# Low halves of split operands and the gate's products moved from GpSimd to VectorE in an attention, mixing and feed-forward kernel

## The chip, the cores and the metric

The kernel runs on one core of one Trainium2 chip. The metric is device time in microseconds from launch to end; three runs of the kernel before took 486.18, 487.32 and 492.7 us, median 487.32 us. The engines are called by their short names: PE (TensorE matmul), PEld (its weight load), DVE (VectorE), ACT (ScalarE), POOL (GpSimd) and SP (the queue that issues all DMAs here).

## The reference

Three stages on 2 batches of 768 tokens, 8 heads of 64, model width 512, all in float32:

```python
# attention: local window of 96 keys plus the first 8 keys, linear distance bias
scores = q @ k^T / 8 - slope[h] * dist
a = softmax(where(is_global | is_local, scores, -1e9));  x = a @ v
# mixing
theta = x @ w_theta;  zr, zi = x * cos(theta), x * sin(theta)
u = x + w_tok_r @ zr + w_tok_i @ zi          # over tokens
x2 = u + max(u @ w_ch, 0)
# feed forward
h = max(x2 @ w_in, 0)                        # width 1024
gate = 1 / (1 + exp(-conv3(h)))              # depthwise over tokens, 3 taps
out = (h * gate) @ w_out
```

## The kernel before

**Numbers.** PE multiplies in a shortened float32 format. So an operand that needs full precision is split: its *high half* is the value copied into that format (`Net.hi`, line 79 on ACT, 81 on POOL, 83 on DVE), its *low half* is the value minus the high half (`Net.lo`, line 87, on POOL or DVE). A product of two split operands is three matmuls: high by high, low by high, high by low. A low half can only be computed once its high half is written. Line 87 is one helper for all of them, so in the profile the tile names tell which split it is.

**Weights** come as float64 and are turned into float32 on the chip, block by block, by a queue of small steps (`Net.weight`, lines 110 to 136): *load* (SP, into one of two buffers `wst`), *a* (ACT, line 95), *b* (DVE, lines 100 and 101), *c* (DVE, lines 107 and 108; afterwards the load buffer is free), *d* (high half, ACT) and *e* (low half, POOL). `advance` (lines 138 to 148) puts the steps of three neighbouring blocks into one queue, and `run(k)` takes k of them out between other work. There are 48 blocks: 4 of `w_theta`, 24 of `w_tok` (384 columns each), 4 of `w_ch`, 8 of `w_in`, 8 of `w_out` (512 columns each).

**The order of the work** is written out by hand: a manual schedule, every engine runs its instructions in the order in which the program emits them and waits at each for what it needs.

- *Attention* (`run_fast`, line 811 on): 48 steps, three per (batch, head), each two tiles of 128 queries. A step emits scores (PE), the biased scores and their row minimum (DVE, line 297), the exponential (ACT), transposes and products with v (PE), each some steps behind the other. Once per head the next head's keys and queries are split (lines 839 and 840): for keys the high half on ACT and the low half on POOL, for queries the high half on DVE and the low half on POOL. Weight steps of `w_theta` and of eight `w_tok` blocks run in between.
- *Mixing* (`Mix.tail`, line 596 on): the angles (`reduce_theta`, lines 456 and 457 on DVE), then for each token tile sine and cosine (ACT), their products with x (DVE, line 470), high halves (DVE) and low halves (POOL) of these: this is `trig`. Then token mixing `tok` in four parts (batch 0 and 1 by first and second half of the outputs, 144 matmuls of 384 columns each), with the rest of the `w_tok` blocks prepared meanwhile; its end adds x (DVE, line 517). Then u is split (`u_split`), and `ch` does the channel mixing in 16 tiles, each with a maximum and sum (DVE, line 542), a high half (ACT) and a low half (POOL).
- *Feed forward*: `ff_in` does 24 matmuls for each of 16 (batch, block of 128 channels). Behind it runs `gate` in stages that a `Pipe` moves by one each time: maximum with 0 into one of three buffers `h` (ACT, line 566); three convolution taps (DVE, lines 568 to 570); sigmoid (ACT, line 572) and its product with h (line 574, POOL for even blocks, DVE for odd ones); high half (ACT) and low half (POOL). A buffer `h` is free again once its product has read it. Last, `ff_out` does 12 tiles of 24 matmuls of 512 columns, batch 0 first, copies them out of PSUM and stores them.

Of the kernel before, what the change touches and what calls it, by code (L numbers as in the profile page):

```python
# [21 lines left out]
P = 128  # L22
# [15 lines left out]
TURN = 6.283185  # the float32 next below 2 pi: half a turn stays inside Sin's range  # L38
# [8 lines left out]
F64_LOW = f32_of_bits(0x38000000)  # high word of the float64 2^-127, read as float32  # L47
F64_HIGH = f32_of_bits(0x47EFFFFF)  # high word of float32's largest value


class Net:
# [41 lines left out]
    def f64_a(self, w, t):  # L93
        """w [P, 2n] int32: pairs of words of float64; t = the high words' magnitudes."""
        self.nc.scalar.activation(t.bitcast(F32), w[:, 1 : w.shape[1] : 2].bitcast(F32), AF.Abs)  # L95

    def f64_b(self, w, t):
        """Into float32's range, and the exponent's and fraction's bits to their places."""
# [4 lines left out]
    def f64_c(self, w, t):  # L103
        """The low word's top bits, the sign and the exponent's top bit."""
# [5 lines left out]
    def weight(self, src, width, hi, lo, eh="A", el="P"):  # L110
        """Queue the load of a block of weights, its conversion and its split. The queue's
        steps are ordered so that a step's inputs come from steps well before it."""
# [25 lines left out]
    def advance(self, n):  # L138
        j = self.jobs

        def put(i, *steps):
            if 0 <= i < len(j):
                self.bg.extend(j[i][x] for x in steps)

        put(n - 1, 1)
        put(n - 2, 2, 3)
        put(n, 0)
        put(n - 2, 4, 5)

    def drain(self):  # L150
        """No more weights soon: queue what the last ones still lack."""
        n = len(self.jobs)
        self.advance(n)
        self.advance(n + 1)
        self.jobs = []
# [11 lines left out]
class Pipe:  # L167
    """Chains of dependent operations, one stage a step, so that no engine waits for
    what another was only just given."""
# [10 lines left out]
    def add(self, *new):  # L180
        """The first stages at once."""
# [14 lines left out]
class Attention:  # L196
    """Attention of one (batch, head) at a time, its inputs split ahead of use."""
# [57 lines left out]
class FastAttention(Attention):  # L255
    """1 <= n_local <= 121 and n_global <= 8: each tile of 128 queries meets the
    120 keys before it, the first 8 keys and its own 128 keys."""
# [6 lines left out]
    def table(self, i):  # L264
        """The head's biases; tile 0's window has its own."""
# [73 lines left out]
class GeneralAttention(Attention):  # L339
    """Any n_global and n_local: every query tile meets all keys."""  # L340
# [44 lines left out]
class Mix:  # L385
    """What follows the attention."""
# [20 lines left out]
    def transpose_x(self, b, c, e="A"):  # L407
        """x^T of a pair of heads, in stages."""
# [9 lines left out]
    def split_xT(self, b, c, el="P"):  # L418
# [6 lines left out]
    def theta(self, t, tag, bufs):  # L425
        """The products of one token tile, one at a time."""
# [11 lines left out]
    def theta1_open(self, t):  # L438
        """Theta of batch 1's token tile t as far as the first three pairs of heads go."""
# [10 lines left out]
    def reduce_theta(self, th, out):  # L450
        """theta in turns, less the nearest whole number of them; in stages."""
# [7 lines left out]
    def trig(self, b, t, r, z, em, eh, el):  # L459
        """z = x cos, x sin of one token tile, split; z: [cos, sin] of [P, hi/lo, DM]; in stages."""  # L460
# [17 lines left out]
    def trig0(self):  # L478
        """x cos and x sin of batch 0, in stages."""
# [3 lines left out]
        for k in range(NT + 2):  # L483
# [4 lines left out]
            if k < NT:  # L488
                tr.append(self.trig(0, k, self.r[:, k], z[k], "VV", "VV", "PP"))
# [5 lines left out]
    def load_tok(self, hf, part, eh="A", el="P"):  # L495
        """Queue the weights of token tiles 2 part, 2 part + 1 (r, i each) for one half of the outputs."""
# [6 lines left out]
    def tok(self, b, hf, m, s, bank):  # L503
        """Add token tile s's part of y^T, rows m."""
# [511 lines left out]
```

## Time and profile before

| What | Value |
|---|---|
| runs (median) | 486.18, 487.32, 492.7 us (487.32) |
| span of the profiled execution, first to last instruction | 484.6 us |
| busy: PE, PEld, DVE, ACT, POOL | 420.3, 388.4, 418.1, 217.2, 251.7 us |
| mean granted TensorE clock | 0.952 of full |

The profile lists one execution by its span alone; its own device time is not among the numbers given, so the span is what its rows are laid against. The span begins with the first instruction and ends with the last, and the median of the runs is 2.7 us above it. "Busy" is the time in which an engine had an instruction under way; a wait inside an instruction (for a port, for instance) counts as busy, a wait for a semaphore before it does not. Times of matmuls overlap, so a row of many is read by its sum and not by one of them.

### The profile page before, as it was taken

Reading aid. Unit: us, or ns where it says so; the run is one execution under the profiler, and the core shown is the slowest. Engines: PE = TensorE matmul, PEld = TensorE weight load, DVE = VectorE, ACT = ScalarE, POOL = GpSimd, SP = SyncE. Lnnn points to the kernel's source line nnn. Section 1 sums busy time; section 2 is a strip of 40 time slices with the busy share of each in tenths; the row PEclk is TensorE's granted clock in tenths of the full one; section 3 lists DMA queues with packets and bytes.
Section 4 is the critical chain, followed back from the end, with each engine's and each line's share of the span. In section 5 each row is a group of like instructions: output and inputs, shape, how many; then the busy total and the mean of one; then the engine's idle time right before and its main releaser. Section 6 shows DMA issues by size and latency. Waiting matters only on the chain.

```text
span 484.6 us, 6636 instructions
## 1 busy us (share of the span) xinstructions
PE 420.3 (87%) x2376; PEld 388.4 (80%) x2376; DVE 418.1 (86%) x700; ACT 217.2 (45%) x420; POOL 251.7 (52%) x164
## 2 busy tenths in 40 slices
PE   3888797889899897799668999679999688999995
PEld 2778797778797797799557999479999688788885
DVE  5989999999998997998788999999999999994000
ACT  3867767556678303902323222544634433443000
POOL 2756666654544742674233285577556675575000
PEclk9979979798999998999998999979999898999999
DMA  6865545534320003102444423312311000003111
GB/s 216 297 219 190 177 158 193 161 133 164 93 67 1 0 1 98 32 1 76 120 131 131 130 88 122 94 45 87 105 38 34 0 1 0 1 0 123 52 43 50
DMA packets 14297, 44.53 MB, mean 92 GB/s; under 512 B 1840, under 2 KB 2352, under 8 KB 14256
## 3 DMA queue, kind: packets, MB, share of 16 engines
q1 hardware_dynamic: 14256, 44.03, 28.1%
q8 instruction: 20, 0.33, 0.3%
q14 instruction: 21, 0.17, 0.1%
HBM read 40.88 MB, written 3.15 MB: 91 GB/s over the span
## 4 chain that ended last, share of the span: by engine, by line
DVE 39%; PE 17%; DMA 6%; issue 4%; ACT 1%; SPq 0%; ACTq 0%; DVEq 0%
PE O L90 6%; DVE wbit L107 5%; DMA wst<-w_tok 4%; DVE wbit L101 4%; PE PT L90 4%; PE S L90 4%; DVE wbit L108 4%; DVE c L569 4%; DVE wbit L100 3%; DVE c L570 3%; DVE r L470 3%; PE X L90 3%; DVE scratch L470 3%; DVE c L568 2%; PE TH L90 2%
## 5 line engine op out<-in xcount | busy, mean ns | idle before, releaser
L87 POOL TENSOR_TENSOR qk<-a,qk 128x768 fp32r<-128x768 f32 (+1 forms) x29 | 58.5, 2017 | 40.7 <-ACT qk L79 27.2
L90 PE MATMUL S<-qk 128*128 128x256 f32 (+1 forms) x192 | 39.5, 332 | 26.3 <-DVE nm L297 10.5
L95 ACT ACTIVATE wbit<-wst 128x512 f32<-128x512 f32 (+1 forms) x48 | 29.4, 616 | 73.0 <-DMA wst<-w_tok 25.5
L90 PEld LDWEIGHTS S<-qk 128*128 128x128 f32 x192 | 31.1, 220 | 31.4 <-issue 13.6
L87 POOL TENSOR_TENSOR wt<-wbit,wt 128x384 fp32r<-128x384 f32 x24 | 27.6, 1150 | 54.2 <-ACT wt L79 54.2
L306 ACT ACTIVATE a<-a,nm 128x256 f32<-128x256 f32 (+1 forms) x96 | 42.0, 484 | 23.9 <-DVE nm L297 23.8
L100 DVE TENSOR_SCALAR wbit<-wbit 128x512 f32<-128x512 f32 (+1 forms) x48 | 40.7, 848 | 7.4 <-ACT wbit L95 7.3
L107 DVE SCALAR_TENSOR_TENSOR wbit<-wst,wbit 128x512 int32<-128x512 int32 (+1 forms) x48 | 45.5, 949 | 1.2
L101 DVE TENSOR_SCALAR wbit<-wbit 128x512 int32<-128x512 int32 (+1 forms) x48 | 44.3, 923 | 1.7
L90 PE MATMUL O<-wt,z 128*128 128x384 f32 x144 | 33.0, 362 | 13.5 <-ACT wt L79 9.0
L90 PEld LDWEIGHTS O<-wt,z 128*128 128x128 f32 x144 | 25.8, 197 | 18.6 <-ACT wt L79 11.5
L87 POOL TENSOR_TENSOR g<-c,g 128x768 fp32r<-128x768 f32 x16 | 34.3, 2148 | 9.9 <-ACT g L79 8.0
L108 DVE SCALAR_TENSOR_TENSOR wbit<-wst,wbit 128x512 int32<-128x512 int32 (+1 forms) x48 | 36.1, 753 | 1.7
L297 DVE CUSTOM_DVE_ANT_0 a<-S,a 128x256 f32<-128x256 f32 (+1 forms) x96 | 34.1, 394 | 1.2 <-PE PT L315 0.8
L79 ACT ACTIVATE wt<-wbit 128x384 fp32r<-128x384 f32 x24 | 12.5, 520 | 44.4 <-DVE wbit L108 44.0
L90 PE MATMUL O<-a,a 128*128 128x65 f32 x236 | 31.9, 280 | 0.0
L574 POOL TENSOR_TENSOR c<-c,scratch 128x768 f32<-128x768 f32 x8 | 18.9, 2364 | 23.4 <-ACT c L572 23.4
L90 PEld LDWEIGHTS O<-a,a 128*128 128x128 f32 x236 | 31.0, 204 | 0.0
L315 PE MATMUL PT<-ident,a 128*128 128x128 f32 x176 | 30.0, 294 | 0.0
L570 DVE SCALAR_TENSOR_TENSOR c<-scratch,cwt,c 128x767 f32<-128x767 f32 x16 | 28.0, 1750 | 0.6
L90 PE MATMUL TH<-wth,xTs 128*128 128x512 f32 x96 | 28.3, 436 | 0.2
L79 ACT ACTIVATE a<-PT 128x512 f32<-128x512 f32 (+1 forms) x48 | 26.2, 546 | 2.8 <-PE PT L315 2.8
(193 smaller groups left out, 1077.2 us busy)
## 6 DMA issues: line engine op xcount, KB each, us to landing
a<-qk SPq DMA_DIRECT2D x14, 792.0 KB, 4.8
wst<-w_tok SPq DMA_DIRECT2D x24, 384.0 KB, 3.1
a<-v SPq DMA_DIRECT2D x16, 357.5 KB, 2.9
wst<-w_in SPq DMA_DIRECT2D x8, 512.0 KB, 3.4
wst<-w_out SPq DMA_DIRECT2D x8, 512.0 KB, 3.5
out<-scratch SPq DMA_DIRECT2D x11, 256.0 KB, 2.6
wst<-w_theta SPq DMA_DIRECT2D x4, 512.0 KB, 5.5
wst<-w_ch SPq DMA_DIRECT2D x4, 512.0 KB, 3.5
```

The source lines that it names most:

```text
L79: self.nc.scalar.activation(out, in_, AF.Copy)
L87: e.tensor_tensor(out, in_, hi.bitcast(F32), op=ALU.subtract)
L90: self.nc.tensor.matmul(out, l, r, start=start, stop=stop)
L95: self.nc.scalar.activation(t.bitcast(F32), w[:, 1 : w.shape[1] : 2].bitcast(F32), AF.Abs)
L100: nc.vector.tensor_scalar(t.bitcast(F32), t.bitcast(F32), F64_LOW, F64_HIGH, op0=ALU.max, op1=ALU.min)
L101: nc.vector.tensor_scalar(t, t, 3, 0x3FFFFFFF, op0=ALU.logical_shift_left, op1=ALU.bitwise_and)
L107: nc.vector.scalar_tensor_tensor(t, lo, 29, t, op0=ALU.logical_shift_right, op1=ALU.bitwise_or)
L108: nc.vector.scalar_tensor_tensor(t, hi, -(1 << 30), t, op0=ALU.bitwise_and, op1=ALU.bitwise_or)
L297: nc.vector.tensor_tensor_reduce(sS[:, c], s["sp"][:, c], self.T[1 if t0 else 0], scale=-0.125, scalar=3.0e38, op0=ALU.add, op1=ALU.min, a ...
L306: self.nc.scalar.activation(sS[:, rng[u]], sS[:, rng[u]], AF.Exp, bias=nm[:, u : u + 1], scale=-1.0)
L315: self.nc.tensor.transpose(pt[:, c], sS[:, c], net.head["ident"])
L570: nc.vector.scalar_tensor_tensor(c[:, 0 : S - 1], h[:, 1:S], cw[:, f, 2:3], c[:, 0 : S - 1], op0=ALU.mult, op1=ALU.add)
```

## The change

Every low half that POOL computed is computed by DVE: the defaults and arguments `"P"` become `"V"`. So are the gate's products of even blocks. POOL keeps what it does once at the start (index patterns, constants). For three kinds of work the low half is also emitted later than before: in the weight queue, step *e* of a block is put at the head of the next `advance` (so `drain` advances once more); in `ch` and in `gate` a `yield` stands between high and low half, which puts the low half one `Pipe` step later. No shape, buffer, tile, DMA or matmul changes. The diff also takes out comments, which moves line numbers by 2 to 4 (the convolution taps are lines 571 to 573 there, the product 577).

```diff
-    def weight(self, src, width, hi, lo, eh="A", el="P"):
+    def weight(self, src, width, hi, lo, eh="A", el="V"):
...
+        put(n - 3, 5)
         put(n - 1, 1)
         put(n - 2, 2, 3)
         put(n, 0)
-        put(n - 2, 4, 5)
+        put(n - 2, 4)
...
         self.advance(n)
         self.advance(n + 1)
+        self.advance(n + 2)
...
-    def split_xT(self, b, c, el="P"):
+    def split_xT(self, b, c, el="V"):
...
-                tr.append(self.trig(0, k, self.r[:, k], z[k], "VV", "VV", "PP"))
+                tr.append(self.trig(0, k, self.r[:, k], z[k], "VV", "VV", "VV"))
...
-    def load_tok(self, hf, part, eh="A", el="P"):
+    def load_tok(self, hf, part, eh="A", el="V"):
...
             n.hi(eh, self.x2[b][0][:, m, c], x2)
+            yield
             n.lo(el, self.x2[b][1][:, m, c], x2, self.x2[b][0][:, m, c])
...
         n.hi(eh, g[:, 0], c)
+        yield
         n.lo(el, g[:, 1], c, g[:, 0])
...
-        tr = [self.trig(1, s, r[s], self.z[1][s], "VV", "VV", "PP") for s in range(NT)]
+        tr = [self.trig(1, s, r[s], self.z[1][s], "VV", "VV", "VV") for s in range(NT)]
...
-        pipe.step(*(self.u_split(0, x, 0, "V", "P") for x in range(KC)))
+        pipe.step(*(self.u_split(0, x, 0, "V", "V") for x in range(KC)))
...
-                    new = [self.ch(b, hf, m, bank(), "A", "P")]
+                    new = [self.ch(b, hf, m, bank(), "A", "V")]
...
-            pipe.step(self.gate(b, f, hs[k % 3], cs[:, k % 4], banks, "PV"[f % 2], "A", "P"))
+            pipe.step(self.gate(b, f, hs[k % 3], cs[:, k % 4], banks, "V", "A", "V"))
...
-                split_q(net, st, qk, "A", "P")
+                split_q(net, st, qk, "A", "V")
             if i > 0 and tp == 0:
-                split_k(net, st, qk, "A", "P")
-                split_q(net, st, qk, "V", "P")
+                split_k(net, st, qk, "A", "V")
+                split_q(net, st, qk, "V", "V")
...
-            last.add(mix.split_xT(b, c, "P" if b else "V"))
+            last.add(mix.split_xT(b, c, "V"))
...
-        net.lo("P", qk0[:, S : 2 * S][:, qc[x]], q[:, qc[x]], qk0[:, qc[x]])
+        net.lo("V", qk0[:, S : 2 * S][:, qc[x]], q[:, qc[x]], qk0[:, qc[x]])
```

Three places show how the change moves instructions. First DVE in `trig` of batch 1 (`r` and `scratch` hold sine and cosine, `z` the split products; `xs` is x), before:

```order
L470 TENSOR_TENSOR r_147<-r_147,xs_134 128x512
L470 TENSOR_TENSOR scratch<-scratch,xs_134 128x512
L83 CAST z_1842<-r_147 128x512
L83 CAST z_1842<-scratch 128x512
L470 TENSOR_TENSOR r_147<-r_147,xs_134 128x512
```

and with the change:

```order
L472 TENSOR_TENSOR r_147<-r_147,xs_134 128x512
L472 TENSOR_TENSOR scratch<-scratch,xs_134 128x512
L83 CAST z_1842<-r_147 128x512
L83 CAST z_1842<-scratch 128x512
L87 TENSOR_TENSOR z_1842<-r_147,z_1842 128x512
L87 TENSOR_TENSOR z_1842<-scratch,z_1842 128x512
L472 TENSOR_TENSOR r_147<-r_147,xs_134 128x512
```

The two low halves now stand between one token tile's high halves and the next tile's products. Second DVE while the `w_tok` blocks of the second output half are prepared (`wbit` is a block under conversion, `wst` its load buffer, `wt` the split weights), before:

```order
L107 SCALAR_TENSOR_TENSOR wbit_2077<-wst_2075,wbit_2077 128x384
L108 SCALAR_TENSOR_TENSOR wbit_2077<-wst_2075,wbit_2077 128x384
L100 TENSOR_SCALAR wbit_2081<-wbit_2081 128x384
L101 TENSOR_SCALAR wbit_2081<-wbit_2081 128x384
L107 SCALAR_TENSOR_TENSOR wbit_2081<-wst_2079,wbit_2081 128x384
```

and with the change:

```order
L107 SCALAR_TENSOR_TENSOR wbit_2077<-wst_2075,wbit_2077 128x384
L108 SCALAR_TENSOR_TENSOR wbit_2077<-wst_2075,wbit_2077 128x384
L87 TENSOR_TENSOR wt_2073<-wbit_2077,wt_2073 128x384
L100 TENSOR_SCALAR wbit_2081<-wbit_2081 128x384
L101 TENSOR_SCALAR wbit_2081<-wbit_2081 128x384
L107 SCALAR_TENSOR_TENSOR wbit_2081<-wst_2079,wbit_2081 128x384
```

The low half of a block stands right behind its last conversion step on DVE, although ACT's copy into the high half lies between the two, and ahead of the next block's conversion. Third DVE in the feed-forward stage once the weights are done (`c` is the convolution, its buffer numbers left equal; `scratch` holds h, `g` the split gate), before:

```order
L568 TENSOR_SCALAR c_3037<-scratch,cwt 128x768
L569 SCALAR_TENSOR_TENSOR c_3037<-scratch,cwt,c_3037 128x767
L570 SCALAR_TENSOR_TENSOR c_3037<-scratch,cwt,c_3037 128x767
L574 TENSOR_TENSOR c_3037<-c_3037,scratch 128x768
L568 TENSOR_SCALAR c_3037<-scratch,cwt 128x768
```

and with the change:

```order
L571 TENSOR_SCALAR c_3035<-scratch,cwt 128x768
L572 SCALAR_TENSOR_TENSOR c_3035<-scratch,cwt,c_3035 128x767
L573 SCALAR_TENSOR_TENSOR c_3035<-scratch,cwt,c_3035 128x767
L577 TENSOR_TENSOR c_3035<-c_3035,scratch 128x768
L87 TENSOR_TENSOR g_3376<-c_3035,g_3376 128x768
L571 TENSOR_SCALAR c_3035<-scratch,cwt 128x768
```

Before, the product stands on DVE behind every second block's taps only; now it stands behind every block's, and behind it the low half of the block two further back.

## Rows read from the trace of the kernel before

**Rows 1.** Page, part 1: busy us, share of the span, instructions.
```profile
PE 420.3 (87%) x2376; PEld 388.4 (80%) x2376; DVE 418.1 (86%) x700; ACT 217.2 (45%) x420; POOL 251.7 (52%) x164
```
**Rows 2.** Page, part 4: the chain that ended last, shares by engine.
```profile
DVE 39%; PE 17%; DMA 6%; issue 4%; ACT 1%; SPq 0%; ACTq 0%; DVEq 0%
```
**Rows 3.** Busy time by stretch: us, PE, PEld, DVE, ACT, POOL, clock, DMA.
```profile
10.00:142.60 132.60, 113.35 (x788) 106.17 (x789) 127.84 (x352) 91.33 (x197) 76.24 (x42) 0.91 0.53 175
...
153.00:218.00 65.00, 58.48 (x301) 54.09 (x301) 61.58 (x80) 23.54 (x42) 37.39 (x27) 0.97 0.08 25
218.00:258.00 40.00, 31.58 (x167) 28.06 (x165) 33.15 (x51) 10.64 (x21) 14.46 (x13) 1.00 0.39 112
258.00:318.00 60.00, 50.47 (x271) 48.31 (x271) 56.94 (x79) 20.38 (x37) 32.28 (x25) 0.95 0.34 105
...
343.50:412.90 69.40, 62.25 (x335) 60.80 (x333) 68.21 (x57) 29.80 (x52) 40.16 (x19) 0.95 0.07 23
```
**Rows 4.** Timeline, gate stage: start us, duration us, engine, line, operation.
```profile
419.18 2.14 POOL L87 TENSOR_TENSOR g<-c,g 128x768 fp32r<-128x768 f32 x1 [0.38 <-ACT g L79]
419.66 2.48 DVE L570 SCALAR_TENSOR_TENSOR c<-scratch,cwt,c 128x767 f32<-128x767 f32 x1
422.07 0.94 DVE L574 TENSOR_TENSOR c<-c,scratch 128x768 f32<-128x768 f32 x1
422.94 0.60 DVE L568 TENSOR_SCALAR c<-scratch,cwt 128x768 f32<-128x768 f32 x1
...
424.63 1.02 DVE L570 SCALAR_TENSOR_TENSOR c<-scratch,cwt,c 128x767 f32<-128x767 f32 x1
```
**Rows 5.** Groups on DVE, attention (10 to 142.6 us): count, busy us, mean ns, idle.
```profile
L267 DVE TENSOR_SCALAR a<-Dt 128x256 f32<-128x256 f32 x16 | 11.4, 710 | 1.0 <-issue 0.5
L100 DVE TENSOR_SCALAR wbit<-wbit 128x384 f32<-128x384 f32 x8 | 9.7, 1211 | 0.0
...
L101 DVE TENSOR_SCALAR wbit<-wbit 128x384 int32<-128x384 int32 x8 | 8.1, 1009 | 0.3
...
L100 DVE TENSOR_SCALAR wbit<-wbit 128x512 f32<-128x512 f32 x4 | 6.8, 1690 | 0.0
```
**Rows 6.** Groups on POOL, the same stretch.
```profile
L87 POOL TENSOR_TENSOR qk<-a,qk 64x816 fp32r<-64x816 f32 x14 | 29.4, 2098 | 30.4 <-ACT qk L79 23.4 <-issue 3.1 <-PE PT L315 2.1
L87 POOL TENSOR_TENSOR qk<-a,qk 128x768 fp32r<-128x768 f32 x15 | 29.1, 1941 | 10.3 <-DVE qk L83 6.0 <-ACT qk L79 3.8
```
**Rows 7.** Timeline, DVE in `trig` of batch 1.
```profile
195.57 0.68 DVE L470 TENSOR_TENSOR r<-r,xs 128x512 f32<-128x512 f32 x1
...
196.78 0.42 DVE L83 CAST z<-r 128x512 fp32r<-128x512 f32 x1
...
197.45 1.78 DVE L470 TENSOR_TENSOR r<-r,xs 128x512 f32<-128x512 f32 x1
...
201.50 1.78 DVE L470 TENSOR_TENSOR r<-r,xs 128x512 f32<-128x512 f32 x1
```
**Rows 8.** Timeline, one `w_tok` block after another, second output half.
```profile
238.18 0.54 ACT L95 ACTIVATE wbit<-wst 128x384 f32<-128x384 f32 x1 [2.64 <-DMA wst<-w_tok]
...
239.15 0.36 DVE L101 TENSOR_SCALAR wbit<-wbit 128x384 int32<-128x384 int32 x1
...
240.81 0.56 DVE L108 SCALAR_TENSOR_TENSOR wbit<-wst,wbit 128x384 int32<-128x384 int32 x1
...
241.40 0.53 ACT L79 ACTIVATE wt<-wbit 128x384 fp32r<-128x384 f32 x1
...
242.01 1.02 POOL L87 TENSOR_TENSOR wt<-wbit,wt 128x384 fp32r<-128x384 f32 x1 [1.65 <-ACT wt L79]
242.19 1.26 DVE L107 SCALAR_TENSOR_TENSOR wbit<-wst,wbit 128x384 int32<-128x384 int32 x1
```
**Rows 9.** Chain of waits, in order of time: end of `ch`, start of `ff_out`.
```profile
332.85 2.09 PE PT L90 x12
...
412.96 11.27 PE O L90 x48
```

More of the change, by code (lines that the diff above doesn't have):

```diff
@@ L724, in tail @@
                 self.tok(1, 1, m, s, pb)
-            pipe.step(*(self.u_split(0, x, 1, "V", "P") for x in range(KC) if m == 0))
+            pipe.step(*(self.u_split(0, x, 1, "V", "V") for x in range(KC) if m == 0))
             n.run(12)
@@ L878, in run_general @@
         split_k(net, st, qk, "V", "P")
-        split_q(net, st, qk, "V", "P")
+        split_q(net, st, qk, "V", "V")
         o = net.bank("O", 2)
```

## The prediction

> **What bounds the kernel now.** I start with the busy times [rows 1]. DVE has something under way in 86% of the span and PE in 87%, but PE's matmuls overlap, and a wait inside one counts as busy, so its share says less. The chain of waits puts 39% on DVE and 17% on PE [rows 2]; the reader is to see that DVE leads and that POOL, busy for 251.7 us, is not on it at all. The table by stretch then says where: DVE is busy 127.8 of 132.6 us in the attention, 61.6 of 65.0 in the stretch with `trig`, 56.9 of 60.0 before and in the channel mixing, 68.2 of 69.4 in the gate stage [rows 3]. Only from 218 to 258 us is nobody full: there the `w_tok` blocks come one after another and the queue of load, ACT and DVE sets the pace. After 412.96 us PE does `ff_out` without a gap [rows 9]; nothing of the change shortens that.
>
> The next question is what DVE's busy time is made of. In the gate stage the timeline shows the same convolution tap taking 2.48 us at 419.66, while a low half runs on POOL from 419.18 for 2.14 us, and 1.02 us at 424.63, with POOL idle [rows 4]. The tap does not run slower beside POOL: its 2.48 are nearly the 1.66 us that POOL still had to go and then its own 1.02. So DVE and POOL take turns whenever both read SBUF this way, and the wait is booked as DVE busy. The same two values appear for the products in `trig` (0.68 and 1.78 us [rows 7]) and for the conversion steps (0.36 alone, means of 1.0 to 1.7 in the attention [rows 8, 5]). That is the whole case for the change: DVE already pays for POOL's work, at POOL's price of about 2.1 us for 768 columns, where DVE itself does a two-input operation of that size in 0.94 us [rows 4, 6].
>
> A rule speaks against it. The Trainium skill (Perfetto Trace Analysis, "Optimizing Scalar/DVE Operations") says that when DVE is saturated, work may be moved off it, even to GpSimd, and adds that the two share a read port, so that it might not help. By its first half the attention alone, where DVE has no room [rows 3], would grow by the 36.2 us of added work that is counted below, and the kernel would take 523 us; the turn-taking in the timeline [rows 4] sides with its second half.
>
> **Part by part.** Durations come from one profiled execution of 484.6 us span; the median of the runs, 487.3, is 2.7 above it. The terms are differences, so I carry them over to the median.
>
> *Attention, 10 to 142.6 us.* POOL's 14 key and 15 query low halves [rows 6] come to DVE: 14 x 1.0 (0.94 scaled to 816 columns) and 15 x 0.94 = 28.1. Eight `w_tok` and four `w_theta` low halves add 8 x 0.56 and 4 x 0.68 (two-input operations of 384 and 512 columns [rows 8, 7]) = 7.2, and one low half of x^T 0.9: 36.2. What goes is the holding [rows 5]: line 267, 11.4 less 16 x 0.36 = 5.6 (0.36 is what 384 columns take alone [rows 8], so a bound for its 256); lines 100 and 101 at 384 columns, 17.8 less 16 x 0.36 = 12.0; line 100 at 512 columns, 6.8 less 4 x 0.48 (0.36 scaled) = 4.9. That is 22.5 in four rows; line 101 at 512 columns, the casts and the low halves of x^T already on DVE are held too and not in it. Independent DVE operations also start before the last one ends: two products take 1.21 us from start to start and 1.36 by duration [rows 7], which takes about 0.07 off each of 43 added ones, 3.0 in all. So the stretch changes by at most 36.2 - 22.5 - 3.0 = +10.7 and by less than nothing if the unlisted forms are held like the listed ones (then they give more than 10.7). I take **0**, nearer to the second end because every held form in the rows loses most of its time, and keep -6 and +10.7.
>
> *`trig` and the blocks around it, 153 to 218 us.* A held token tile takes 4.05 us on DVE (197.45 to 201.50). With the change it is two products in 1.21, two casts in 0.67 (196.78 to 197.45), two low halves like the products, 1.21: 3.09 [rows 7]. That is 0.96 less. Twelve tiles pass here; some, like the one at 195.57, are not held now and gain nothing on DVE, but the held first tile of batch 1 also lets PE start earlier. I count seven: **-6.7**, with ends of -3 (few held) and -9.
>
> *`w_tok` blocks of the second half, 218 to 258 us.* Here the change adds a wait. On DVE the low half stands directly behind line 108, and it needs ACT's copy: 108 ends at 241.37, the copy ends at 241.93, POOL starts at 242.01, so 0.64 us pass in which DVE stands still, and behind it stands the next block's conversion, and behind that the next load, which needs the buffer. Then the low half itself, 0.56. Now DVE goes ahead at once and is held instead for 1.26 - 0.56 = 0.70 [rows 8]. So a turn costs 1.20 in place of 0.70, 0.5 more; two blocks are under way, so twelve blocks are six turns, and the first has its loads early: 5 x 0.5 = 2.5, less two holds of 0.70 that the first pair loses. **+1.1**, ends -1 and +5. Nothing on SP moves past anything: the queue of steps keeps its order, the low half only changes its place from the end of one `advance` to the head of the next.
>
> *258 to 318 us.* DVE would do twelve 512-column blocks at 2 x 0.48 and 3 x 0.68 (3.0 each, 36.0), nine sums of `tok` at 0.56 (5.0), eight casts at 0.3 (a 512-column one follows the next by 0.33 [rows 7]; 2.4), fourteen low halves of u and x2 at 0.56 (7.8), five of line 542 (2.8) and small ones (1.3): 55.3, less 0.07 x 85 = 6.0 for overlap. Six handovers of 0.64, where the low half stands directly behind 108, give +3.8, and its idle 3.1 [rows 3] stays: 56.2 against 60. The loads can set the pace instead (ACT waits 2.64 for one [rows 8]), so I take less than the 3.8: **-1.5**, ends -5 and +4.
>
> *318 to 343.5 us.* Low halves of x2 and `w_out` come in, holds go out: 0.
>
> *Gate stage.* Now DVE goes from its first tap at 343.5, where I cut the stretch, to the product of block 9 at its end; then ACT can fill that block's h again, its PSUM bank comes free and `ff_out` starts at 412.96. With the change a block's taps take 1.69 from the first's start to the third's (422.94 to 424.63) and 1.02, so 2.71; the product 0.87 (422.07 to 422.94), a low half of the same size the same [rows 4]. Up to that product stand 11 blocks' taps, 10 products, 8 low halves, four `w_out` blocks of 3.0 and the low half of a fifth: 29.8 + 8.7 + 7.0 + 12.7 = 58.2, so it is done at 401.7, and ACT's 0.5 or so later `ff_out` can start. PE says about the same: `ff_in` starts at 334.94 and needs 16 x 24 matmuls at 2.09 per 12, 66.9 us, so until 401.8 [rows 9]. Against 412.96 that is **-10.6**, ends -5 (if handovers to ACT stall the gate) and -11.1 (PE's floor). The extra stage of the pipe costs nothing: batch 1's last low half is needed only when six tiles of `ff_out`, 33 us at 11.27 for two [rows 9], are done.
>
> Sum: 0 - 6.7 + 1.1 - 1.5 - 10.6 = -17.7, so **469.6 us** (span near 467).
>
> **The rivals.**
> (a) *The attention pays.* The listed holds are most of what there is, and the key low half waits for ACT's copy of the keys once per head. Then the attention costs +8, the `w_tok` blocks +5 in place of +1.1: 481. For it: the listed rows cover 22.5 of 36.2 only. Against: every DVE form that I looked at and that reads SBUF shows two values. Within 2%; chance 0.14.
> (b) *The attention gains too.* If all forms are held like those in rows 5 and overlap is full, its -6 and two more in 258 to 318 make 462. Chance 0.14.
> (c) *Slower: DVE inherits POOL's waits.* ACT takes the next block's line 95 before it copies the last block, and line 95 waits for a load (2.64 us [rows 8]). Where DVE has other work ready at that moment, in the 24 blocks of 512 columns after the attention, the low half holds all of it up for 2.64 in place of 0.64: 24 x 2.0 = 48, so 517 or 518. Nine such blocks use up the gain; at 14, 28 us, it is slower by 2%. For it: in-order DVE and POOL's long waits for ACT [rows 6]. Against: loads start when DVE frees a buffer, two steps ahead, and the blocks stand further apart where other work is emitted between. Chance 0.07.
> (d) *No relief: the long durations are not POOL's doing*, so that added work adds up: 523 from the attention alone. It is where the rule's first half would lead. Against it rows 4. Chance 0.03.
>
> **How the numbers follow.** My forecast has 0.62. Within 2% means 477.6 to 497.1, about what a measurement of this kernel can tell from no change. The forecast's own ends leave 0.02 of it above 477.6; so faster 0.60 + 0.14 = 0.74; within 2% 0.02 + 0.14 + 0.01 (a weak (c)) = 0.17; slower 0.06 + 0.03 = 0.09. The range goes from 457 (b with its ends) to 481 (the middle of a): it leaves out (c), (d), half of (a) and the end of (b), 0.2.
>
> **What would show it.** Right: POOL has nothing after its first microseconds; line 100, 101 and the taps show one value each (0.36 to 0.48, 1.02); DVE's busy time falls to about 400 although it has some 150 more instructions; `ff_in` runs without a gap and `ff_out` starts near 395; a token tile of `trig` takes 3.1 us. Wrong: taps over 1.1 us without POOL; DVE idle behind ACT's copies for more than 20 us in sum; an attention that ends later than 150 us; a gap on PE before `ch` of batch 1 that grows by more than what was won before it.

## The result, and the profile after

The changed kernel takes 467.17 us (median of four runs, 465.49 to 469.67), the kernel before beside it 486.75: a ratio of 0.9588 (95% interval 0.9522 to 0.9653), 20 us less. The profiled execution has a span of 463.6 us in place of 484.6. A second profiled execution of the changed kernel (e5) has 462.9 us at a mean granted clock of 0.961 (0.981 in the first, 0.952 before), so the gain does not hang on the clock's mean. Executions of one kernel differ by up to some 1.5%, in e9 with the clock that they were granted (452.1 to 453.5 us at 0.981 to 0.984, 458.8 to 459.2 at 0.966 to 0.973), and all ratios, and the times given for e7 and e9, leave out those more than 1.5% above the kernel's fastest.

Parts 1 and 4 of the page after, to lay beside [rows 1, 2]:

```profile
PE 411.5 (89%) x2376; PEld 380.5 (82%) x2376; DVE 383.3 (83%) x854; ACT 217.6 (47%) x420; POOL 1.4 (0%) x10
...
DVE 46%; PE 37%; DMA 7%; ACT 4%; issue 3%; SPq 0%; ACTq 0%; DVEq 0%
```

DVE executes 154 instructions more and is busy 34.8 us less. The shares of the chain must not be laid side by side: before, it could be followed back only to 153.9 us (its shares add up to 67%), after to 8.9. From the second tile of `trig` on, which both cover, DVE has 187 us of the chain before and 101 after, PE 83 and 154; behind the gate's first tap DVE has 65 us before and 0.4 after. DVE no longer leads everywhere.

Where the 21.0 us of the span come from, by landmark instructions (us; the end of the last row minimum and of the last conversion step, the start of the last product of `trig` and of the first matmul of `ff_in` and `ff_out`):

| Stretch | before | after | difference |
|---|---|---|---|
| start to the last row minimum of the attention | 142.64 | 144.89 | +2.3 |
| to the start of the last product of `trig` | 72.9 | 64.9 | -8.0 |
| to the last conversion step of `w_tok` | 42.3 | 41.4 | -0.9 |
| to the start of `ff_in` | 77.0 | 74.0 | -2.9 |
| `ff_in`, to the start of `ff_out` | 78.2 | 67.2 | -11.0 |
| to the end | 71.6 | 71.2 | -0.4 |

The last product of `trig` was itself held before (1.77 us) and is not after (0.69). To its end, `trig` gains 9.1 us and the `w_tok` blocks lose 0.2.

The groups on DVE in the attention, for [rows 5] and the added low halves:

```profile
L87 DVE TENSOR_TENSOR qk<-a,qk 64x816 fp32r<-64x816 f32 x15 | 15.1, 1005 | 0.7 <-ACT qk L79 0.3
L87 DVE TENSOR_TENSOR qk<-a,qk 128x768 fp32r<-128x768 f32 x15 | 14.4, 959 | 0.5
...
L269 DVE TENSOR_SCALAR a<-Dt 128x256 f32<-128x256 f32 x15 | 4.4, 294 | 0.5
...
L101 DVE TENSOR_SCALAR wbit<-wbit 128x384 int32<-128x384 int32 x8 | 2.9, 360 | 0.3
L100 DVE TENSOR_SCALAR wbit<-wbit 128x384 f32<-128x384 f32 x8 | 2.8, 353 | 0.0
...
L100 DVE TENSOR_SCALAR wbit<-wbit 128x512 f32<-128x512 f32 x4 | 1.7, 423 | 0.0
```

The held forms fell to what they take alone (1211 to 353 ns, 1690 to 423). That pays for the 29.5 us of key and query low halves: the four rows of [rows 5] give back about 24 us, and forms that they leave out some more (line 101 at 512 columns 7.7 to 1.7 us, the low halves of x^T 8.2 to 3.8).

The gate stage's timeline on DVE, for [rows 4], and the chain of waits there, for [rows 9]:

```profile
363.28 0.61 DVE L571 TENSOR_SCALAR c<-scratch,cwt 128x768 f32<-128x768 f32 x1
363.93 1.02 DVE L572 SCALAR_TENSOR_TENSOR c<-scratch,cwt,c 128x767 f32<-128x767 f32 x1
364.98 1.02 DVE L573 SCALAR_TENSOR_TENSOR c<-scratch,cwt,c 128x767 f32<-128x767 f32 x1
365.91 0.95 DVE L577 TENSOR_TENSOR c<-c,scratch 128x768 f32<-128x768 f32 x1
366.78 0.95 DVE L87 TENSOR_TENSOR g<-c,g 128x768 fp32r<-128x768 f32 x1
```

```profile
390.42 2.12 PE PT L90 x12
392.54 11.02 PE O L90 x48
```

A block's five operations take 4.4 us with both taps at 1.02, and PE goes from `ff_in` to `ff_out` without a gap. The table by stretch (columns as in [rows 3]) shows the same, and where somebody is still not full:

```profile
10.00:142.60 132.60, 110.96 (x779) 101.86 (x780) 125.26 (x381) 90.66 (x194) 0.00 (x0) 0.96 0.52 174
153.00:212.40 59.40, 58.05 (x310) 54.25 (x310) 55.30 (x110) 25.74 (x46) 0.00 (x0) 1.00 0.09 28
212.40:252.00 39.60, 31.27 (x169) 28.50 (x167) 28.45 (x62) 11.20 (x23) 0.00 (x0) 1.00 0.40 113
...
335.50:392.50 57.00, 57.00 (x327) 57.00 (x326) 55.64 (x73) 30.52 (x51) 0.00 (x0) 1.00 0.07 22
```

In the `w_tok` blocks DVE is busy 28.5 of 39.6 us. The timeline there shows the wait that the change added, for [rows 8] (in brackets the idle time before, and who ended it):

```profile
217.43 0.55 ACT L95 ACTIVATE wbit<-wst 128x384 f32<-128x384 f32 x1 [2.69 <-DMA wst<-w_tok]
217.88 0.51 ACT L79 ACTIVATE wt<-wbit 128x384 fp32r<-128x384 f32 x1
218.42 0.56 DVE L87 TENSOR_TENSOR wt<-wbit,wt 128x384 fp32r<-128x384 f32 x1 [1.24 <-ACT wt L79]
```

ACT takes the next block's line 95 first, which waits for its load; the copy of the finished block stands behind it, and DVE behind that. The wait is not 1.24 us each time: over the whole kernel DVE waits 12.7 us in 16 waits for ACT's copies of `w_tok`, 18.5 us with those of other weights and of the keys and queries.

### The profile page after: what moved, and what is told of

The parts are those of the page before. It is cut to its first block, busy times and chain, and to the rows that moved or that the text cites. A ratio compares the mean times of both kernels' runs of the same rounds, so it can differ in the third digit from the quotient of the medians.

```text
span 463.6 us, 6488 instructions
## 1 busy us (share of the span) xinstructions
PE 411.5 (89%) x2376; PEld 380.5 (82%) x2376; DVE 383.3 (83%) x854; ACT 217.6 (47%) x420; POOL 1.4 (0%) x10
## 4 chain that ended last, share of the span: by engine, by line
DVE 46%; PE 37%; DMA 7%; ACT 4%; issue 3%; SPq 0%; ACTq 0%; DVEq 0%
PE O L90 11%; PE S L90 8%; PE PT L90 8%; DVE qk L87 6%; DVE a L299 6%; PE X L90 5%; DVE wbit L107 4%; PE TH L90 4%; DMA wst<-w_tok 3%; DVE wbit L108 3%; DVE z L87 3%; DMA wst<-w_in 3%; DVE wbit L101 2%; DVE wbit L100 2%; DVE qk L83 2%
## 5 line engine op out<-in xcount | busy, mean ns | idle before, releaser
L90 PE MATMUL O<-wt,z 128*128 128x384 f32 x144 | 30.1, 345 | 9.5 <-ACT wt L79 9.5
L108 DVE SCALAR_TENSOR_TENSOR wbit<-wst,wbit 128x512 int32<-128x512 int32 (+1 forms) x48 | 30.0, 625 | 1.7
L107 DVE SCALAR_TENSOR_TENSOR wbit<-wst,wbit 128x512 int32<-128x512 int32 (+1 forms) x48 | 30.0, 624 | 1.5
L87 DVE TENSOR_TENSOR qk<-a,qk 64x816 fp32r<-64x816 f32 (+1 forms) x30 | 29.5, 982 | 1.2 <-ACT qk L79 0.3
L90 PE MATMUL TH<-wth,xTs 128*128 128x512 f32 x96 | 26.0, 408 | 0.5 <-ACT r L456 0.2
L90 PE MATMUL PT<-wt,z 128*128 128x384 f32 x132 | 25.8, 335 | 0.0
L87 DVE TENSOR_TENSOR wt<-wbit,wt 128x384 fp32r<-128x384 f32 x24 | 13.3, 556 | 12.7 <-ACT wt L79 12.7
L90 PEld LDWEIGHTS PT<-wt,z 128*128 128x128 f32 x132 | 23.2, 188 | 0.0
L317 PEld LDWEIGHTS PT<-ident,a 128*128 128x128 f32 x176 | 22.4, 151 | 0.7 <-ACT a L79 0.7
L90 PE MATMUL S<-wt,z 128*128 128x384 f32 x120 | 22.3, 337 | 0.5 <-DVE z L87 0.5
L90 PEld LDWEIGHTS S<-wt,z 128*128 128x128 f32 x120 | 20.9, 188 | 0.8 <-DVE z L87 0.8
```

Source lines behind the costliest of these rows:

```text
L87: e.tensor_tensor(out, in_, hi.bitcast(F32), op=ALU.subtract)
L90: self.nc.tensor.matmul(out, l, r, start=start, stop=stop)
L107: nc.vector.scalar_tensor_tensor(t, lo, 29, t, op0=ALU.logical_shift_right, op1=ALU.bitwise_or)
L108: nc.vector.scalar_tensor_tensor(t, hi, -(1 << 30), t, op0=ALU.bitwise_and, op1=ALU.bitwise_or)
L317: self.nc.tensor.transpose(pt[:, c], sS[:, c], net.head["ident"])
```

## The experiments

The theory: while a two-input operation ran on POOL, DVE was *held* (its instruction was under way but waited), and the gain is the holding that goes, mostly in `trig` and the gate. The rivals: the later emission is the gain; or it comes from the gate alone; or the long durations on DVE were not POOL's. The stages of every profiled execution, by the landmarks of the table above (one execution each, us):

| Kernel | row minimum | `trig` | `w_tok` | to `ff_in` | `ff_in` | ratio to before (95%) |
|---|---|---|---|---|---|---|
| before | 142.6 | 72.9 | 42.3 | 77.0 | 78.2 | 1 |
| after, again (e5) | 144.6 | 65.7 | 41.2 | 72.9 | 67.2 | 0.9568 (0.9496 to 0.9640) |
| e1, gate only | 142.5 | 72.9 | 42.8 | 76.3 | 67.9 | 0.9793 (0.9753 to 0.9833) |
| e2, delay only | 143.0 | 73.0 | 42.2 | 76.9 | 79.0 | 1.0024 (0.9993 to 1.0055) |
| e3, no delay | 145.7 | 64.9 | 41.4 | 80.3 | 68.4 | 0.9734 (0.9703 to 0.9766) |
| e4, POOL load | 144.8 | 65.7 | 41.4 | 73.0 | 78.2 | one run, 476.39 us |
| e6, attention on POOL | 146.1 | 64.9 | 41.1 | 73.0 | 67.2 | 0.9485 (0.9445 to 0.9524) |
| e7, low half later | 154.6 | 64.7 | 36.3 | 68.6 | 67.2 | 0.9462 (0.9389 to 0.9535) |
| e8, `trig` only | 143.8 | 65.2 | 40.3 | 76.7 | 78.5 | 0.9798 (0.9756 to 0.9841) |
| e9, later after the attention | 143.7 | 70.3 | 36.1 | 68.3 | 67.2 | 0.9278 (0.9208 to 0.9349) |
| e10, e9 with attention on POOL | 143.4 | 64.7 | 36.1 | 68.2 | 67.2 | 0.9276 (0.9211 to 0.9341) |
| e11, delay in the queue only | 143.6 | 69.7 | 41.2 | 74.6 | 70.4 | 0.9649 (0.9577 to 0.9721) |

**e1: the gate alone.** The kernel before, with

```diff
         n.hi(eh, g[:, 0], c)
+        yield
         n.lo(el, g[:, 1], c, g[:, 0])
...
-            pipe.step(self.gate(b, f, hs[k % 3], cs[:, k % 4], banks, "PV"[f % 2], "A", "P"))
+            pipe.step(self.gate(b, f, hs[k % 3], cs[:, k % 4], banks, "V", "A", "V"))
```

> The kernel before with one part of the change: only the gate's low halves and its even products go to DVE (with the later stage for the low half); all other low halves stay on POOL. Theory (DVE was held for about 2.1 us by each of POOL's operations; the gate stage alone gains 10.6 us because PE becomes its bound): ff_in takes 67 us in place of 78, all stretches before it as before, so about 476 us. The low halves of w_out that stay on POOL in the first half of that stage may keep 1 to 3 us of it (477 to 479). Rival 1 (the gate is where nearly all of the 20 us came from): 468 to 471. Rival 2 (the gain is in the later emission alone): the gate's share is the same with the engine left as it was, which the next kernel tells.

476.8 us; `ff_in` 67.9 us, all stretches before it as before. The gate is half of the gain, as the theory has it.

**e2: the later emission alone.** The kernel before with the three changes of place (`yield` as in e1, another in `ch`, and the queue), all low halves still on POOL:

```diff
+        put(n - 3, 5)
         put(n - 1, 1)
         put(n - 2, 2, 3)
         put(n, 0)
-        put(n - 2, 4, 5)
+        put(n - 2, 4)
```

> The kernel before with the later emission alone: the low half at the head of the next block's steps in the weight queue, one stage later in the channel mixing and in the gate, all of it still on POOL. Theory (POOL was off the chain of waits, and what it cost was the holding, which does not depend on when it is emitted): 0 to within 3 us, so 484 to 490 us, with conversion steps and taps on DVE still showing two values each. Rival (a good part of the 20 us is the delay): 470 to 480.

488.59 us, no change. A gain by the delay itself is out.

**e3: DVE without the delay.** The changed kernel with e2's three edits undone (its signs turned round), all low halves on DVE.

> The changed kernel with the later emission undone: every low half on DVE, but directly behind its high half. Theory: in the gate stage DVE then stands still behind ACT's copy of the high half, about 0.9 us in each of some 11 blocks, in a stage where DVE has 1.4 us to spare beside PE: +8 to +10 us there; in the channel mixing 16 tiles with about 0.6 us each, partly covered: +2 to +5; in the weight queue DVE's order is the same with and without the delay, so nothing: 477 to 482 us in all, and DVE's busy time as in the changed kernel (383 us). Rival (delay is the gain): 485 or more. Rival (the handover is covered by PE's queue): 467.

474.17 us. The sum is 3 us under the theory's range and its parts were wrong: 1.2 us in the gate, not 8 to 10, and 6.3 before it, not 2 to 5, most of that through the queue, where the theory had put nothing (e11). In the gate ACT makes sigmoid and copy while DVE does the next block's taps. Before `ff_in`, a wait of PE (5.4 us; 2.1 in the changed kernel) and a piece of DVE's timeline:

```profile
PE TH L90 <- DVE xT L517: 5.4, 1, 5.4
```

```profile
300.16 0.69 DVE L108 SCALAR_TENSOR_TENSOR wbit<-wst,wbit 128x512 int32<-128x512 int32 x1
302.21 0.69 DVE L87 TENSOR_TENSOR win<-wbit,win 128x512 fp32r<-128x512 f32 x1 [1.36 <-ACT win L79]
302.82 0.55 DVE L517 TENSOR_TENSOR xT<-TH,xT 128x384 f32<-128x384 f32 x1
```

The low half of a `w_in` block waits for ACT, and the sum of `tok` that PE needs stands behind it. The change's place in the queue lets such sums pass.

**e11: which delay pays.** The changed kernel without the two `yield`s, the queue as changed:

```diff
             n.hi(eh, self.x2[b][0][:, m, c], x2)
-            yield
             n.lo(el, self.x2[b][1][:, m, c], x2, self.x2[b][0][:, m, c])
...
         n.hi(eh, g[:, 0], c)
-        yield
         n.lo(el, g[:, 1], c, g[:, 0])
```

> The changed kernel with the later emission kept in the weight queue and undone in the channel mixing and in the gate. Without all three the kernel took some 7 us more, 6.3 of them between the w_tok blocks and ff_in, 1.2 in the gate. Theory (in the gate and in the channel mixing ACT copies while DVE does the next block's taps or the next tile's maximum, so the wait is covered; what pays is the queue, where PE waited 5.4 us for line 519 behind a low half of w_in): 465 to 469 us. Rival (the channel mixing's own stage pays): 471 to 475.

471.29 us, which by its total is the rival; by stage it is neither. In its profiled execution 4.8 us of the difference stand in `trig`, where its instructions are those of the changed kernel (the clock, below). To `ff_in` it lost 0.6 (1.7 beside e5), so most of e3's loss of 6.3 there was the queue. `ff_in` lost 3.2, at its start, where these rows stand (ACT, ACT, DVE):

```profile
325.07 0.66 ACT L95 ACTIVATE wbit<-wst 128x512 f32<-128x512 f32 x1 [2.60 <-DMA wst<-w_out]
325.63 0.93 ACT L79 ACTIVATE x<-scratch 128x384 fp32r<-128x384 f32 x2
...
326.18 0.56 DVE L87 TENSOR_TENSOR x<-scratch,x 128x384 fp32r<-128x384 f32 x1 [1.85 <-ACT x L79]
```

ACT's copy of x2 stands behind line 95 and its load, DVE's low half behind that, and once more at 333.93 with 2.00 us: the prediction's rival (c). Both stand in `ch`, so it is that `yield` that keeps them away; the two were not taken out one by one.

**e4: POOL made busy again, with nobody waiting.** In `ff_in`, on a tile nobody uses (`gh`: half of a finished high half of the gate):

```diff
+            if k >= 4:
+                gh = self.g[(k - 4) // NF][(k - 4) % NF][:, 0, 0:HALF].bitcast(F32)
+                if k < 8:
+                    for _ in range(4):
+                        self.nc.gpsimd.tensor_tensor(spare, gh, gh, op=ALU.subtract)
+                elif k < 12:
+                    for _ in range(4):
+                        self.nc.gpsimd.tensor_copy(spare, gh)
...
+                    for _ in range(4):
+                        self.nc.gpsimd.memset(spare, 0.0)
```

> The changed kernel with work for POOL that nobody waits for, in the gate stage only: in each of blocks 4 to 7 four subtractions of 384 columns that read a finished high half twice and write a spare tile, in blocks 8 to 11 four copies of that size, in blocks 12 to 15 four memsets of it. Theory (POOL's two-input operations hold DVE): beside the subtractions (1.02 us each) taps and products on DVE show 1.5 to 3 us in place of 1.02 and 0.95, and the four blocks take 10 to 16 us longer; so the span is 474 to 480 in place of 463.6. Beside the copies it is open: as long as they run if a read of SBUF is what excludes DVE (some 2 us a block), nothing if a second operand is needed; beside the memsets nothing. Rival (the long durations before came from what DVE and POOL share as operands, or from a wait for a semaphore): no operand is rewritten and nobody waits here, so all forms keep one value and the span stays at 464 to 466.

474.6 us span, `ff_in` 11.0 us longer. By the starts of the blocks' first taps on DVE, the blocks with subtractions took 8.5 us longer (the theory had 10 to 16), those with copies 3.4, those with memsets nothing. The span lies in the theory's range only because the copies add what the subtractions lack. POOL's groups, and the two engines' timelines beside subtractions, a copy and memsets:

```profile
L775 POOL TENSOR_TENSOR Dt<-g 128x384 f32<-128x384 f32 x16 | 18.1, 1133 | 353.9 <-ACT g L79 352.9
L778 POOL COPY Dt<-g 128x384 f32<-128x384 f32 x16 | 16.7, 1041 | 8.1 <-ACT g L79 7.3
L782 POOL MEMSET Dt<- 128x384 f32 x14 | 5.9, 419 | 1.0 <-POOL Dt L780 0.2
```

```profile
372.12 1.46 DVE L572 SCALAR_TENSOR_TENSOR c<-scratch,cwt,c 128x767 f32<-128x767 f32 x1
372.85 1.42 POOL L775 TENSOR_TENSOR Dt<-g 128x384 f32<-128x384 f32 x1
373.62 1.46 DVE L573 SCALAR_TENSOR_TENSOR c<-scratch,cwt,c 128x767 f32<-128x767 f32 x1
...
380.11 1.26 DVE L577 TENSOR_TENSOR c<-c,scratch 128x768 f32<-128x768 f32 x1
380.61 1.12 POOL L778 COPY Dt<-g 128x384 f32<-128x384 f32 x1
381.29 1.25 DVE L87 TENSOR_TENSOR g<-c,g 128x768 fp32r<-128x768 f32 x1
...
402.28 0.95 DVE L87 TENSOR_TENSOR g<-c,g 128x768 fp32r<-128x768 f32 x1
```

A tap takes 1.46 in place of 1.02 beside subtractions, a low half 1.25 in place of 0.95 beside copies, and nothing is added beside memsets, which read nothing. No operand is shared with them and nobody waits for POOL, so POOL's reading of SBUF is what holds DVE: rival (d) is out. The ends of the operations show that the two engines take turns, each held by the other. The subtraction that starts at 372.85 ends at 374.27, 0.69 us behind the tap that ends at 373.58; the tap that starts at 373.62 ends at 375.08, 0.81 behind that subtraction. All 16 subtractions end 0.68 or 0.69 us behind the end of an operation on DVE, all 16 copies 0.36 or 0.37; the memsets show no such distance. So POOL's listed means (1133 and 1041 ns) contain its own waits for DVE, and DVE lost only what POOL still had to go at its start, less 0.1 to 0.2: 0.44 of 0.65 us for the tap, 0.30 of 0.44 for the low half. That is the prediction's reading of [rows 4], where 1.66 us were to go and the tap took 1.46 longer.

**e8: `trig` alone.** The kernel before with

```diff
-                tr.append(self.trig(0, k, self.r[:, k], z[k], "VV", "VV", "PP"))
+                tr.append(self.trig(0, k, self.r[:, k], z[k], "VV", "VV", "VV"))
...
-        tr = [self.trig(1, s, r[s], self.z[1][s], "VV", "VV", "PP") for s in range(NT)]
+        tr = [self.trig(1, s, r[s], self.z[1][s], "VV", "VV", "VV") for s in range(NT)]
```

> The kernel before with one part of the change: the low halves of the products with sine and cosine on DVE. Theory: a token tile takes 3.1 us in place of 4.05 and the last product of the stretch ends 5 to 7 us earlier (215.6 before), of which the w_tok blocks behind it keep most: 479 to 483 us. Rival 1 (the 6 us of that stretch came from the weight blocks or from the attention's other end): 486 or more. Rival 2 (the loads of the w_tok blocks were issued by then and take the gain back): the last product earlier, but 484 to 488 us.

478.01 us, a little better than forecast; the stretch is 7.7 us shorter and the blocks behind it keep all of it. The ratios of e1 and e8 (-2.1% and -2.0%) add up to the change's -4.1%: what it does in the attention, the weight blocks and the channel mixing is nothing in sum, as far as the intervals tell (some 4 us).

**e6: the attention back on POOL.**

```diff
-                split_k(net, st, qk, "A", "V")
-                split_q(net, st, qk, "V", "V")
+                split_k(net, st, qk, "A", "P")
+                split_q(net, st, qk, "V", "P")
```

and likewise for x^T of batch 1, `w_theta` and the first eight `w_tok` blocks.

> The changed kernel with the attention's low halves back on POOL (keys, queries, x^T of batch 1, the four w_theta and the first eight w_tok blocks), all later ones on DVE. Theory (the attention is a break-even: 35.6 us of added low halves against 37.0 us that the held forms lose, summed from the groups of both traces): the last row minimum ends 1 to 3 us earlier than in the changed kernel (144.9 us), everything behind it is as there, so 463 to 467 us, no more than 0.5% from the changed kernel; conversion steps in the attention show two values again and none after 155 us. Rival 1 (the attention pays for the change): 455 to 460. Rival 2 (the attention gained too, and the later end is chance): 471 to 476.

462.81 us beside the changed kernel's 464.66 (e5):

> The changed kernel as it is, as the reference of the three kernels beside it: 465 to 470 us, ratio to the kernel before 0.952 to 0.965 as measured.

The intervals overlap: no difference is shown. By this pair alone POOL could be better there by up to some 8 us; e9 and e10 below, the same pair once more, differ by nothing. That the row minimum would end earlier was a miss (146.1). It ends between 143.6 and 145.7 in five other kernels with DVE there and between 142.5 and 143.8 in five others with POOL, so the +2.3 of the first table is not established either.

**e7: the low half later in the queue.**

```diff
-        put(n - 3, 5)
         put(n - 1, 1)
         put(n - 2, 2, 3)
         put(n, 0)
         put(n - 2, 4)
+        put(n - 3, 5)
```

> The changed kernel with the low half of a weight block queued two steps further back: behind the next block's conversion and its copy instead of ahead of it, so that DVE never has it next while ACT, which takes the load of the block after it first, has not copied yet. Theory (the 18.5 us that DVE stands behind ACT's copies of weights sit in a circle of load, ACT, DVE while the second half's w_tok blocks are prepared, 12 blocks at 3.37 us): the waits of line 87 for wt, win and wch fall below 4 us in sum; a block takes 2.9 us, and the stretch from 212 to 252 us loses 4 to 6 us; 461 to 464 us. Rival 1 (the loads set the pace there, DVE's idle time only changes its name): 466 to 468, with ACT's waits for the loads longer by what DVE's are shorter. Rival 2 (w_tok's last low halves come later and PE waits for them instead): 468 to 472.

461.8 us. The mechanism held: `w_tok` 36.3 us, DVE no longer waits for a copy there. But the attention ends 9.7 us later, which neither the theory nor a rival had. One row of ACT there, and one of DVE:

```profile
96.86 0.55 ACT L95 ACTIVATE wbit<-wst 128x384 f32<-128x384 f32 x1 [3.50 <-DVE wth L87]
```

```profile
96.14 0.68 DVE L87 TENSOR_TENSOR wth<-wbit,wth 128x512 fp32r<-128x512 f32 x1
```

The low half reads one of three conversion buffers; where the steps are taken one to three at a time between other work, a later low half keeps the buffer from ACT's line 95, and ACT, with the exponentials behind it, stands still (7.9 us in five such waits up to 156 us; none in the changed kernel). Not all of the 9.7 us is this: the granted clock fell to 0.50 between 140 and 150 us in this execution. Beside e9, whose clock fell as far just behind the attention (last section), the last product of `trig` starts 5.3 us later (219.2 and 213.9), and that is about what is left for the buffer.

**e9, e10: later after the attention only.** The changed kernel with

```diff
-        put(n - 3, 5)
+        if not self.late:
+            put(n - 3, 5)
...
         put(n - 2, 4)
+        if self.late:
+            put(n - 3, 5)
...
     net.drain()
+    net.late = True
     mix.alloc_xTs()
```

where the flag is set once the twelve blocks of the attention are queued. e10 has e6's edits as well.

> The changed kernel with the low half of a weight block queued behind the next block's conversion, as in the kernel that did so for all blocks, but for the 36 blocks after the attention only; the twelve in it stay as the change has them. Theory (the later place takes DVE's waits for ACT away where blocks follow one another closely; in the attention it kept the conversion buffers taken, ACT stood at line 95 behind them, and the exponentials behind that): the attention ends as in the changed kernel (last row minimum 145 us, not 154.6), the 12 blocks of the second half take 36.3 us and the rest to ff_in 68.6, as measured there: ff_in starts near 315 and the kernel takes 453 to 457 us. Rival 1 (the attention's 9.7 us were given back because later blocks came closer after a later start, so that only the sum counts): 461 to 465. Rival 2 (the waits move to PE behind w_tok's low halves): 459 to 462.

> As the kernel beside it, and with the attention's low halves back on POOL. Theory (the attention is a break-even): within 0.5% of the kernel beside it, 451 to 459. Rival (POOL in the attention is better by the 1.9 us that the medians of an earlier comparison differed by, or by more): 449 to 452.

453.1 and 452.1 us, equal ratios. The attention's loss is gone and the rest stays; both beat the changed kernel, with intervals that lie apart from e5's. A pair of blocks in e10 (its lines are one higher: 96 is line 95):

```profile
215.69 0.55 ACT L96 ACTIVATE wbit<-wst 128x384 f32<-128x384 f32 x1 [2.65 <-DMA wst<-w_tok]
...
217.75 0.57 ACT L96 ACTIVATE wbit<-wst 128x384 f32<-128x384 f32 x1 [1.09 <-DMA wst<-w_tok]
...
221.41 0.55 ACT L96 ACTIVATE wbit<-wst 128x384 f32<-128x384 f32 x1 [2.64 <-DMA wst<-w_tok]
```

Two blocks take 5.72 us, 2.9 each, as e7's theory has it, where the changed kernel took 3.37. The longer `trig` stretch of e9's profiled execution goes with its clock (last section).

## Why the prediction was right

It said 469.6 us; the median was 467.2. Its case, DVE pays for POOL's work, is shown by e4, and that the gain is not the delay by e2. One reading under it was too wide: that POOL is not on the chain of waits at all holds only from 153.9 us on, as far back as that chain goes, and the attention is not in it. Of its signs of being wrong one came near: DVE stands idle behind ACT's copies for 18.5 us, the mark was 20. The terms:

- *Attention: 0 forecast, +2.3 in this trace, no difference shown by e6 and e10.* The unlisted held forms were what decided between its ends: line 101 at 512 columns alone went from 7.7 to 1.7 us.
- *`trig`: -6.7 forecast, -8.0 to the start of its last product and -9.1 to its end, -7.7 alone in e8.* A tile takes 3.08 us as worked out, but the count behind the sum was wrong in both directions, so that its size came out is in part luck. From one tile's first product to the next, five gaps lost 1.0 us each. Three grew, by 1.2, 1.2 and 0.7 us, where the prediction had no change: a tile that was not held now has its low halves in its own turn (195.57 to 197.45 in [rows 7], 191.88 to 194.99 here). The other 6.2 us went elsewhere: 3.0 between the last two tiles of batch 0 (there line 456 fell from 1.51 to 0.42 us), 2.1 from there to batch 1's first tile, 1.1 in the last tile's first product. In the timeline:

```profile
191.88 0.69 DVE L472 TENSOR_TENSOR r<-r,xs 128x512 f32<-128x512 f32 x1
...
194.99 0.68 DVE L472 TENSOR_TENSOR r<-r,xs 128x512 f32<-128x512 f32 x1
...
198.06 0.69 DVE L472 TENSOR_TENSOR r<-r,xs 128x512 f32<-128x512 f32 x1
```

- *`w_tok` blocks: +1.1 forecast; -0.9 in the table, +0.2 from the end of `trig`'s last product, +0.9 over nine blocks by their pace* (3.27 us a block before, 3.37 after, by the starts of line 95). The sign holds, but both prices in the term were too low. A handover, taken as 0.64 behind line 108 from one row, is 0.83 on average (9.1 us in 11 waits) and 1.24 where a load stands before the copy. And holding went from every block, not from every pair: line 107 fell from 1118 to 559 ns on average and line 101 from 524 to 360, 0.7 us a block. e9 shows what the wait itself costs: about 5 us.
- *258 to 318: -1.5 forecast, -3.4 measured (318.03 before, 308.00 after, less 6.6 won by then).* The worked-out -3.8 was right and the discount for loads was not needed.
- *Gate: -10.6 forecast, -11.0 measured; alone 10.3 in e1.* PE's floor sets the end, as worked out: 66.9 forecast, 67.2 measured, and DVE has gone from the chain there.

Of the rivals, (a) and (b) are not borne out: in e6 and e10 moving the attention's low halves shows no difference. (d) is out by e4. (c), the slower one, was right in its mechanism and wrong in its count: DVE does inherit waits for loads through ACT (1.24 in the changed kernel, 1.85 and 2.00 in e11), but a stall behind a weight's copy lasts 0.4 to 1.3 us in the changed kernel and not 2.64, and the places that would have held up PE are those that the delays take care of.

The Trainium skill (Perfetto Trace Analysis, "Optimizing Scalar/DVE Operations") says that DVE and GpSimd share a read port, so that moving work between them might not help. e4 agrees: 11.0 us were lost to POOL work that nobody waits for. The Trainium skill (SBUF — State Buffer, "SBUF: two separate sides") calls the pair of ports that the two share an exclusive lock: whichever starts first has it for its whole instruction, and the other is blocked. The fixed distances in e4 (0.69 and 0.36 us from the end of DVE's operation to the end of POOL's, 0.81 from there to the end of DVE's next tap) agree.

## What to carry to other kernels

Before work is put on POOL to relieve a full DVE, look whether one form on DVE shows two durations: here the longer one was DVE's wait for its turn, that is POOL's work paid by DVE. When such work is brought back behind another engine's result, look at what that engine does first, and place it where nothing urgent stands behind it and no scarce buffer hangs on it: here the move was worth 20 us and the place another 10 (by the stages of e9 beside e5) to 14 (by the ratios).

## What the runs showed of the hardware

An operation on POOL that reads SBUF and one of the held forms on DVE (two operands in SBUF, or lines 100 and 101) took turns, each held by the other, and the wait is listed as duration on both. In the kernel before, POOL's low halves of 768 columns in the gate end 1.69 to 1.71 us behind the DVE operation that held them, and a tap ends 0.82 us behind POOL ([rows 4]: 421.32 and 422.14); in [rows 8] line 107 ends 0.42 us behind POOL's low half of 384 columns (243.03 and 243.45). Memsets on POOL held none of the two-operand operations beside them (1.02 and 0.95 us, as alone) and were not held (419 ns). DVE's row minimum, which reads PSUM, shows no hold either: 416 ns on average in the attention before, where POOL was busy 76.2 of 132.6 us, and 419 after.

TensorE's granted clock at the end of the attention fell in some executions and not in others. The table by stretch of e9, and of e10:

```profile
140.00:145.00 5.00, 3.83 (x23) 3.69 (x24) 4.89 (x16) 3.49 (x9) 0.00 (x0) 0.76 0.21 66
145.00:150.00 5.00, 5.00 (x26) 5.00 (x26) 3.35 (x6) 3.45 (x7) 0.00 (x0) 0.50 0.00 0
```

```profile
140.00:145.00 5.00, 4.70 (x44) 4.56 (x43) 4.93 (x14) 4.53 (x12) 3.12 (x2) 1.00 0.30 80
145.00:150.00 5.00, 5.00 (x38) 4.64 (x37) 4.05 (x10) 4.82 (x8) 3.65 (x2) 1.00 0.01 2
```

In e9 it was 0.50 (1.2 GHz) from 145 to 155 and had begun to fall in the 5 us before, in which PE was busy 3.83 us; in e10 it stayed at 1.00 (2.4 GHz), with PE busy 4.70. The stretch that follows takes 70.3 and 64.7 us. e11 has the same drop (0.52 and 0.50 from 145 to 155) and much the same stretch, 69.7 us. But in the first execution of the changed kernel the clock stayed at 1.00 with PE busy 3.72 of the same 5 us. What decides whether the clock falls there stays open.
